# 64x64 array tiles for the chunk products of an RWKV-7 recurrence, and state products that alternate array halves

## The chip, the cores and the metric

The kernel runs on one core of a Trainium2 chip. The metric is the device time of one execution in microseconds. The core has TensorE (PE, matrix products; its weight loads are listed as PEld), VectorE (DVE), ScalarE (ACT), GpSimd (POOL) and SyncE (SP, which issues the DMAs). Products land in PSUM, a memory of 128 partitions in 8 banks of 512 fp32 words, and DVE or ACT bring them from there into the main on-chip memory.

## The reference

Two blocks stand in a row. The first is a recurrence over 768 tokens, for 4 batches of 8 heads with a state of 40 by 40 each; the second is a two-layer MLP with an exact gelu on its output, 3072 tokens of 320 values. All is float32.

```python
def _attn_ref(r, k, v, w, a, b):                      # (4, 8, 768, 40) each
    state = np.zeros((B, H, D, D), dtype=np.float32)
    for t in range(S):
        y[:, :, t] = np.einsum('bhd,bhde->bhe', rt, state)
        Sa = np.einsum('bhde,bhe->bhd', state, at)
        state_decay = state * wt[:, :, None, :] - np.einsum('bhd,bhe->bhde', Sa, bt)
        state = state_decay + np.einsum('bhd,bhe->bhde', vt, kt)
    return y

def _moe_ref(x, w_in, w_out):                         # (3072, 320), (320, 2048), (2048, 320)
    h = x @ w_in
    g = 0.5 * h * (1.0 + erf(h * inv_sqrt2))
    return g @ w_out
```

## The kernel before

The recurrence is cut into chunks of C = 64 tokens. A step handles one chunk of two batches: tokens of the first batch lie on partitions 0 to 63, those of the second on 64 to 127. There are 12 chunks and two pairs of batches, so 24 steps, which take turns between the pairs.

A step has two parts. `prep` (L256) needs no state: it scales a, k, b by the decays, turns five arrays so that heads and their columns lie on the partitions (`turn`, L236: four transposes into one PSUM bank and one copy), and multiplies them into token-by-token matrices (`products`, L247): P from bT and aT, A from kT and aT, RV from vT and rT. Then it inverts I + P by blocks, in six levels of z (L284), u (L293) and a transpose T (L301), with a DVE or ACT operation behind each. `chain` (L320) needs the state: X = A v plus a product with the state (`from_state`, L314), sa = the inverse times X, the new state out of Q (L348, ks with v and bs with sn), then M (`products` again, of snT and rT) and Y = RV ks + the state product + M bs.

Heads come in pairs: the first head of a pair lies on array rows 0 to 63, the second on rows 64 to 127, each with 40 values and 24 rows of zeros. `products` takes one half e of the rows after the other. For each it asks for a PSUM bank, multiplies the four pairs q on 64 rows with 128 weight columns and 128 streamed columns, and lets DVE copy the whole bank into place through a mask (L253). Weight columns and streamed columns are the 64 tokens of both batches, so half of each product pairs tokens of different batches; the mask leaves these out, and the tiles that they would go to hold zeros. Q is alike: its two halves e are the two batches, 64 rows each, and one half's eight products stand ahead of the other's. `from_state` uses all 128 rows and 64 weight columns, the two batches again one after the other.

PSUM is split into pools: `ps_prep` and `ps_chain` have three banks each, `ps_fc` two. A bank is free for its next user when the last reader of its contents is done.

The MLP of two chunks is written as a generator of parts (ph, L405, and po, L412), of which `parts` (L427) runs one behind each of the first eight yields of `prep`. Its passes are independent of the current step, and the framework orders each engine's instructions at build time by a model of their durations: it moves MLP passes into places where it expects TensorE to wait. On the chip, each engine's order is then fixed. For the first steps DVE also converts the MLP's weights from float64 words (L202 to L208).

Of the kernel before, what the change touches and what calls it, by code (L numbers as in the profile page):

```python
# [11 lines left out]
INT32 = mybir.dt.int32  # L12
# [5 lines left out]
#: As a float32, the high word of float64's 2 ** -126.  # L18
# [4 lines left out]
def kernel(  # L23
# [12 lines left out]
    """The recurrence in chunks of C = 64 tokens, all in float32.  # L36

    A step is one chunk of two batches, which lie on partitions 0-63 and 64-127; the
    two pairs of batches take turns. Within a chunk, with al[t] the sum of log w from
    the chunk's middle to (not including) t, per column e of the state,  # L40

        a'[t] = a[t] exp(al[t])    k'[s] = k[s] exp(-al[s + 1])    b'[s] = b[s] exp(-al[s + 1])

    and S the state at the chunk's start, decayed to its middle:

        sa[t] = S a'[t] + sum over s < t of v[s] (k'[s] a'[t]) - sa[s] (b'[s] a'[t])
        y[t] = exp(al[t]) (r[t] S + sum over s < t of (r[t] v[s]) k'[s] - (r[t] sa[s]) b'[s])

    The first is a unit triangular system (I + P) sa = X. Its inverse is built exactly,
    by blocks of 1, 2, 4 .. 32 that join in pairs. Arrays with heads on partitions hold  # L50
    two heads, each in 64 rows with zeros behind its D.

    al is at most 32 steps' log w, so the factors, and the products that the masks leave
    out, are finite for any decays above 0.26, and those of this kind are 0.85 to 0.95.
    """
# [22 lines left out]
    def bank(pool, name):  # L78
        return pool.tile([P, 512], FP32, tag=pool.name, name=name)
# [4 lines left out]
    def by_pair(t):  # L84
        return t.rearrange("p (q x) -> p q x", q=NP)
# [100 lines left out]
    def weights(dst, src):  # L186
        """The exponent loses its bias' difference, 7 * 128, in bits 7 to 9, and the 20 bits
        of mantissa in the high word move up; below float32's normal range it is zero. The
        low word, times the power of two that it counts in, is added: one rounding."""
# [57 lines left out]
    def products(pool, dst, lT, rT, mask):  # L247
        for e in range(2):
            rows = slice(e * HP, (e + 1) * HP)
            pt = by_pair(bank(pool, "prod_ps"))  # L250
            for q in range(NP):
                nc.tensor.matmul(pt[:, q], lT[rows, q], rT[rows, q], start=True, stop=True)  # L252
            nc.vector.copy_predicated(  # L253
                dst[:, e], mask.bitcast(INT32).unsqueeze(1).to_broadcast([P, NP, P]), pt)

    def prep(i):  # L256
# [17 lines left out]
        # Tt is the transpose of (I + P)^-1 within blocks of m tokens, and T that of Tt.  # L274
# [39 lines left out]
    def from_state(o, xT, st):  # L314
        for e in range(2):
            rows = slice(e * C, (e + 1) * C)
            for q in range(NP):
                mm(o[rows, 2 * q:2 * q + 2], xT[:, q, rows], st(e, q), False)

    def chain(i):  # L320
# [18 lines left out]
        if c < NCH - 1:  # L339
            f = f_ring(i)  # L340
            for e in range(2):
                rows = slice(e * HP, (e + 1) * HP)
                nc.gpsimd.tensor_tensor(f[rows, :, :, e], half_w[rows, :, 1],
                                        decays[i + NG][2][rows, :, 0], ALU.mult)
            new = st_ring(i)
            for e in range(2):
                rows = slice(e * C, (e + 1) * C)
                Q = bank(ps_chain, "Q")[:, :NP * 2 * D].rearrange("p (q x d) -> p q x d", q=NP, x=2)  # L348
                for q in range(NP):
                    hs = slice(2 * q, 2 * q + 2)  # L350
                    for n, (l_, r_) in enumerate(((ks, v_), (bs, sn))):
                        mm(Q[:, q], l_[rows, hs].rearrange("p h d -> p (h d)"), r_[rows, hs, :D],
                           q == 0 and n == 0)
                ns = new[:, e, :, :, :D]
                fb = f[:, :, e].unsqueeze(3).to_broadcast([P, NP, 2, D])
                if state is None:
                    nc.vector.tensor_tensor(ns, Q, fb, ALU.mult)
                else:
                    nc.vector.tensor_tensor(ns, Q, st[:, e, :, :, :D], ALU.add)
                    nc.vector.tensor_tensor(ns, ns, fb, ALU.mult)  # L360
# [62 lines left out]
    # Parts of the MLP stand between the levels of the inverse, as the tensor engine would  # L423
    # wait there for others.
# [62 lines left out]
```

## Time and profile before

| | |
|---|---|
| time, median of 2 runs | 1968.95 us (1968.61 to 1969.3) |
| span of the profiled execution, first to last instruction | 1934.2 us |
| TensorE busy, matmuls | 1882.7 us |
| VectorE busy | 547.5 us |
| ScalarE busy | 385.4 us |
| GpSimd busy | 127.6 us |

The profiled execution has no time of its own beside its span; the runs' median is 34.8 us above that span. On the page, line numbers such as L252 are those of the kernel above. A line can be that of a helper: L88 is the helper `mm`, which issues the products of X, sa, Q and Y, and they are told apart by the tile that they write. The shape of a product is written as rows * weight columns, then rows x streamed columns; "x16" is a count. The granted clock is the share of TensorE's full clock that the chip let through. The chain is followed back from the last instruction to what released each one.

### The profile page before, as it was taken

What the parts mean: (1) busy time and instruction counts of PE and PEld (TensorE: products, weight loads), DVE (VectorE), ACT (ScalarE), POOL (GpSimd) and SP (SyncE); (2) the same over time, 40 slices, a digit from 0 to 9 for tenths busy, and PEclk for the clock granted to TensorE, in tenths of its full rate; (3) what the DMA queues carried; (4) which work ended last, traced back from release to release, by engine and by line L of the source; (5) the groups of instructions that cost most, each with busy time, mean ns of one, the idle gap of its engine ahead of it and who ended that gap; (6) DMA issues with size and microseconds to landing.
All of it is one profiled execution on the core that took longest, in us unless ns stands there. A gap on an engine that the chain in (4) does not pass through costs nothing.

```text
span 1934.2 us, 28576 instructions
## 1 busy us (share of the span) xinstructions
PE 1882.7 (97%) x12648; PEld 1611.3 (83%) x12648; DVE 547.5 (28%) x1002; ACT 385.4 (20%) x652; POOL 127.6 (7%) x214
## 2 busy tenths in 40 slices
PE   6888899999999999999999999999999999999999
PEld 6888887888888888788788888888888888888785
DVE  2464732322222222133132232222222222232210
ACT  3111112221212212222122122221221221221200
POOL 4121210000000000000000000000000000000000
PEclk9555759987998996998998899899999999999999
DMA  5241310100001001011010010010100100000000
GB/s 87 50 92 49 79 21 8 22 18 11 15 15 21 11 18 21 1 25 24 1 25 14 11 21 17 13 22 7 18 15 11 17 5 11 4 1 7 1 4 11
DMA packets 160905, 39.84 MB, mean 21 GB/s; under 512 B 153424, under 2 KB 156816, under 8 KB 160784
## 3 DMA queue, kind: packets, MB, share of 16 engines
q1 hardware_dynamic: 160784, 38.03, 10.0%
q8 instruction: 99, 1.62, 0.3%
q14 instruction: 22, 0.18, 0.0%
HBM read 34.08 MB, written 3.93 MB: 20 GB/s over the span
## 4 chain that ended last, share of the span: by engine, by line
PE 96%; DVE 2%; POOL 1%; issue 0%; ACT 0%; POOLq 0%
PE ph L405 16%; PE z_ps L284 14%; PE u_ps L293 13%; PE po L412 11%; PE prod_ps L252 9%; PE Y L88 8%; PE T_ps L301 6%; PE Q L88 5%; PE X L88 3%; PE sa L88 2%; PE turned_ps L375 1%; PE sums L226 1%; PE snT_ps L239 1%; PE aT_ps L239 1%; PE kT_ps L239 1%; PE cum L218 1%
## 5 line engine op out<-in xcount | busy, mean ns | idle before, releaser
L405 PE MATMUL ph<-xT,w_in_sb 128*128 128x256 f32 (+1 forms) x1152 | 333.2, 412 | 0.0
L293 PEld LDWEIGHTS u_ps<-zs,T 128*128 128x128 f32 x1920 | 245.1, 206 | 42.4 <-issue 40.3
L293 PE MATMUL u_ps<-zs,T 128*128 128x64 f32 x1920 | 254.7, 290 | 17.5 <-DVE zs L287 17.5
L405 PEld LDWEIGHTS ph<-xT,w_in_sb 128*128 128x128 f32 (+1 forms) x1152 | 188.4, 190 | 99.2 <-issue 86.7
L284 PEld LDWEIGHTS z_ps<-Tt,P 128*128 128x128 f32 x1920 | 244.4, 205 | 19.3 <-issue 14.6
L287 DVE TENSOR_TENSOR zs<-z_ps,level_m 128x512 f32<-128x512 f32 x144 | 99.5, 691 | 553.0 <-PE z_ps L284 553.0
L302 ACT COPY T<-T_ps 128x512 f32<-128x512 f32 x240 | 130.0, 588 | 608.7 <-PE T_ps L301 606.9
L284 PE MATMUL z_ps<-Tt,P 128*128 128x64 f32 x1920 | 249.9, 287 | 0.0
L412 PE MATMUL po<-w_out_sb,gt 128*128 128x320 f32 x768 | 238.9, 443 | 0.0
L412 PEld LDWEIGHTS po<-w_out_sb,gt 128*128 128x128 f32 x768 | 135.2, 192 | 38.5 <-issue 0.3
L296 DVE TENSOR_TENSOR Tt<-u_ps,Tt 128x512 f32<-128x512 f32 x120 | 83.0, 692 | 287.9 <-PE u_ps L293 287.9
L301 PEld LDWEIGHTS T_ps<-ident,Tt 128*128 128x128 f32 x960 | 114.6, 148 | 42.3 <-issue 19.9
L301 PE MATMUL T_ps<-ident,Tt 128*128 128x128 f32 x960 | 137.6, 290 | 12.4 <-DVE Tt L296 12.1
L407 ACT ACTIVATE gt<-ph 128x512 f32<-128x512 f32 x96 | 57.3, 597 | 392.8 <-PE ph L405 392.8
L88 PE MATMUL Q<-sn,bs 64*128 64x80 f32 x352 | 73.2, 328 | 0.0
L277 POOL COPY Tt<-ident 128x1024 f32<-128x1024 f32 x24 | 24.9, 1038 | 684.2 <-PE sa L88 664.8
L88 PE MATMUL Q<-v,ks 64*128 64x80 f32 x352 | 69.8, 320 | 0.0
L88 PEld LDWEIGHTS Q<-sn,bs 64*128 64x128 f32 x352 | 61.8, 231 | 4.7 <-issue 4.3
L376 ACT COPY turned<-turned_ps 128x512 f32<-128x512 f32 x44 | 24.5, 588 | 197.2 <-PE turned_ps L375 197.2
L88 PE MATMUL Y<-bs,M 128*128 128x40 f32 x384 | 62.5, 333 | 0.0
L88 PEld LDWEIGHTS Y<-bs,M 128*128 128x128 f32 x384 | 59.7, 244 | 2.6 <-issue 1.2
L88 PE MATMUL Y<-ks,RV 128*128 128x40 f32 x384 | 59.0, 322 | 0.0
(113 smaller groups left out, 1917.4 us busy)
## 6 DMA issues: line engine op xcount, KB each, us to landing
gt<-in_moe_w_out_dram SPq DMA_DIRECT2D x16, 320.0 KB, 2.9
w_raw<-in_w_dram SPq DMA_DIRECT2D x48, 80.0 KB, 2.8
k_raw<-in_k_dram SPq DMA_DIRECT2D x48, 80.0 KB, 2.8
a_raw<-in_a_dram SPq DMA_DIRECT2D x48, 80.0 KB, 2.8
b_raw<-in_b_dram SPq DMA_DIRECT2D x48, 80.0 KB, 2.8
v<-in_v_dram SPq DMA_DIRECT2D x48, 80.0 KB, 2.6
r<-in_r_dram SPq DMA_DIRECT2D x48, 80.0 KB, 2.8
gt<-in_moe_w_in_dram SPq DMA_DIRECT2D x12, 320.0 KB, 3.1
```

The source lines that it names most:

```text
L88: nc.tensor.matmul(o, lhsT, rhs, start=first, stop=True, skip_group_check=True)
L239: nc.tensor.transpose(by_pair(pt)[:, q], src(q), ident)
L252: nc.tensor.matmul(pt[:, q], lT[rows, q], rT[rows, q], start=True, stop=True)
L284: nc.tensor.matmul(cols(z[:, h]), Pm[:, e, q], right(ident if n == 0 else Tt[:, h]), start=True, stop=True)
L287: nc.vector.tensor_tensor(zs, z, level_m[:, n].unsqueeze(1).to_broadcast([P, H, C]), ALU.mult)
L293: nc.tensor.matmul(u[:, h], T[:, h], zs[:, h], start=True, stop=True)
L296: nc.vector.tensor_tensor(Tr, cols(u.rearrange("p h c -> p (h c)")), Tr, ALU.add)
L301: nc.tensor.transpose(pt[:, q], Tt[:, e * NP + q], ident)
L302: nc.scalar.copy(T[:, e * NP:(e + 1) * NP], pt)
L405: nc.tensor.matmul(ph[:, x], w_in_sb[:rows, kt, (f + x) * P:(f + x + 1) * P], xt[:rows, kt], start=kt == 0, stop=kt == NK - 1)
L407: nc.scalar.activation(gt[:, f:f + 2], ph, ACT.Gelu)
L412: nc.tensor.matmul(po, gt[:, f, j * P:(j + 1) * P], w_out_sb[:, f], start=f == 0, stop=f == NF - 1)
```

## The change

In `products`, both banks are asked for at the start. Each product of 64 rows by 128 weight columns by 128 streamed columns becomes two of 64 by 64 by 64, one for each batch g, and the blocks that pair different batches are not computed any more. Rows e and weight columns g choose one of four 64x64 tiles of the array, and the four take turns within a pair q. The two masked copies of 128 partitions by 512 become four of 64 partitions by 256, behind all matmuls.

In `from_state` the loops change places, so that the two batches alternate. In `chain`, both banks of Q are asked for at the start, the loop over e goes innermost, and the operations on the new state stand behind all of Q's products. All other lines of the difference remove comments.

```diff
     def products(pool, dst, lT, rT, mask):
+        pts = [by_pair(bank(pool, "prod_ps")) for _ in range(2)]
+        for q in range(NP):
+            for g in range(2):
+                own = slice(g * C, (g + 1) * C)
+                for e in range(2):
+                    rows = slice(e * HP, (e + 1) * HP)
+                    nc.tensor.matmul(pts[e][own, q, own], lT[rows, q, own], rT[rows, q, own],
+                                     start=True, stop=True, skip_group_check=True)
         for e in range(2):
-            rows = slice(e * HP, (e + 1) * HP)
-            pt = by_pair(bank(pool, "prod_ps"))
-            for q in range(NP):
-                nc.tensor.matmul(pt[:, q], lT[rows, q], rT[rows, q], start=True, stop=True)
-            nc.vector.copy_predicated(
-                dst[:, e], mask.bitcast(INT32).unsqueeze(1).to_broadcast([P, NP, P]), pt)
+            for g in range(2):
+                own = slice(g * C, (g + 1) * C)
+                nc.vector.copy_predicated(
+                    dst[own, e, :, own],
+                    mask[own, own].bitcast(INT32).unsqueeze(1).to_broadcast([C, NP, C]), pts[e][own, :, own])
...
     def from_state(o, xT, st):
-        for e in range(2):
-            rows = slice(e * C, (e + 1) * C)
-            for q in range(NP):
+        for q in range(NP):
+            for e in range(2):
+                rows = slice(e * C, (e + 1) * C)
                 mm(o[rows, 2 * q:2 * q + 2], xT[:, q, rows], st(e, q), False)
...
             new = st_ring(i)
-            for e in range(2):
-                rows = slice(e * C, (e + 1) * C)
-                Q = bank(ps_chain, "Q")[:, :NP * 2 * D].rearrange("p (q x d) -> p q x d", q=NP, x=2)
-                for q in range(NP):
-                    hs = slice(2 * q, 2 * q + 2)
-                    for n, (l_, r_) in enumerate(((ks, v_), (bs, sn))):
-                        mm(Q[:, q], l_[rows, hs].rearrange("p h d -> p (h d)"), r_[rows, hs, :D],
+            Qs = [bank(ps_chain, "Q")[:, :NP * 2 * D].rearrange("p (q x d) -> p q x d", q=NP, x=2)
+                  for _ in range(2)]
+            for q in range(NP):
+                hs = slice(2 * q, 2 * q + 2)
+                for n, (l_, r_) in enumerate(((ks, v_), (bs, sn))):
+                    for e in range(2):
+                        rows = slice(e * C, (e + 1) * C)
+                        mm(Qs[e][:, q], l_[rows, hs].rearrange("p h d -> p (h d)"), r_[rows, hs, :D],
                            q == 0 and n == 0)
+            for e in range(2):
+                Q = Qs[e]
                 ns = new[:, e, :, :, :D]
...
```

More of the change, by code (lines that the diff above doesn't have):

```diff
@@ L345, in chain @@
             new = st_ring(i)
-            for e in range(2):
-                rows = slice(e * C, (e + 1) * C)
-                Q = bank(ps_chain, "Q")[:, :NP * 2 * D].rearrange("p (q x d) -> p q x d", q=NP, x=2)
-                for q in range(NP):
-                    hs = slice(2 * q, 2 * q + 2)
-                    for n, (l_, r_) in enumerate(((ks, v_), (bs, sn))):
-                        mm(Q[:, q], l_[rows, hs].rearrange("p h d -> p (h d)"), r_[rows, hs, :D],
-                           q == 0 and n == 0)
+            Qs = [bank(ps_chain, "Q")[:, :NP * 2 * D].rearrange("p (q x d) -> p q x d", q=NP, x=2)
[6 more added lines that the diff above has]
+                        mm(Qs[e][:, q], l_[rows, hs].rearrange("p h d -> p (h d)"), r_[rows, hs, :D],
+                           q == 0 and n == 0)
+            for e in range(2):
+                Q = Qs[e]
                 ns = new[:, e, :, :, :D]
```

## The prediction

> **What bounds the kernel now.** I read the page first, for the engine that carries the time, its clock and the chain that ended last.
>
> ```profile
> span 1934.2 us, 28576 instructions
> PE 1882.7 (97%) x12648; PEld 1611.3 (83%) x12648; DVE 547.5 (28%) x1002; ACT 385.4 (20%) x652; POOL 127.6 (7%) x214
> ...
> PEclk9555759987998996998998899899999999999999
> ...
> PE 96%; DVE 2%; POOL 1%; issue 0%; ACT 0%; POOLq 0%
> PE ph L405 16%; PE z_ps L284 14%; PE u_ps L293 13%; PE po L412 11%; PE prod_ps L252 9%; PE Y L88 8%; PE T_ps L301 6%; PE Q L88 5%; PE X L88 3%; PE sa L88 2%; PE turned_ps L375 1%; PE sums L226 1%; PE snT_ps L239 1%; PE aT_ps L239 1%; PE kT_ps L239 1%; PE cum L218 1%
> ```
>
> TensorE is the bound: 96% of the chain, with DVE at 28%. The products (L252) are 9% of it, Q 5%, and X and Y, of which the state products are a third, 11%. The row of the clock says that TensorE often ran slowed. Two stretches of the table by windows (time, then busy us of PE, PEld, DVE, ACT, POOL, then the granted clock) show where:
>
> ```profile
> 0.00:300.00 300.00, 259.82 (x1402) 243.51 (x1403) 141.39 (x325) 54.67 (x90) 64.21 (x119) 0.64 0.28 62
> 300.00:1934.00 1634.00, 1622.85 (x11248) 1367.78 (x11246) 406.10 (x678) 330.69 (x562) 63.41 (x95) 0.95 0.07 13
> ```
>
> The clock takes two values here, 1.0 and 0.5, so 0.64 and 0.95 mean some 216 and 163 us at half clock, 380 in all. Behind the start TensorE is busy 99%.
>
> Then the chain of waits in order of time (start, us, work), for one step at full clock, one at half clock and the levels of the inverse:
>
> ```profile
> 1578.75 2.90 PE Q L88 x28
> ...
> 1583.22 1.64 PE prod_ps L252 x16
> 1584.86 4.85 PE Y L88 x48
> ...
> 1590.93 1.64 PE prod_ps L252 x16
> 1592.57 0.59 PE kT_ps L239 x4
> 1593.16 0.44 PE vT_ps L239 x4
> 1593.60 0.51 PE rT_ps L239 x4
> 1594.11 3.06 PE prod_ps L252 x31
> 1597.16 1.93 PE z_ps L284 x16
> ```
>
> ```profile
> 1047.29 5.42 PE Q L88 x28
> ...
> 1056.70 3.02 PE prod_ps L252 x16
> ```
>
> ```profile
> 1625.87 2.16 PE po L412 x8
> 1628.03 1.73 PE z_ps L284 x16
> ...
> 1633.88 0.71 PE X L88 x12
> ```
>
> Each fp32 product stands as two passes (a weight load and a matmul): 8 products of a call are 16 rows. Prices of a pass: po streams 320 columns in 2.16 / 8 = 0.270 us, 0.84 ns a column. z streams 64 but loads 128 columns of weights, and takes 1.73 / 16 = 0.108 us, again 0.84 ns a column, of the load. So a pass costs the longer of its load and its stream. Behind products z costs 1.93: a change of tile shape is 0.2 us. At half clock the products' 1.64 becomes 3.02.
>
> Whether two halves of the array work at once is seen in the timeline of Q, whose two halves meet only in the middle:
>
> ```profile
> 1579.86 0.27 PE L88 MATMUL Q<-v,ks 64*128 64x80 f32 x1
> 1579.87 0.33 PE L88 MATMUL Q<-sn,bs 64*128 64x80 f32 x1
> 1579.97 0.27 PE L88 MATMUL Q<-v,ks 64*128 64x80 f32 x1
> ```
>
> They do: a pass of the other half starts 0.01 us behind the first, and the first half goes on 0.11 later. The overlap is short today because one half's passes all stand ahead of the other's.
>
> **The change, part by part** (times at full clock, per step; 24 steps, of which 22 have a state).
>
> Products: 16 passes of 128 columns become 32 of 64 by 64, on four tiles. A pass is then 64 x 0.84 = 0.054 us, a tile has 8, so four tiles side by side need 0.43. With the change of shape (0.2) and the first load (0.1) a call is 0.73 at best. No row shows four tiles at once. From above, the densest row is X with 12 passes in 0.71, 0.059 a pass, so 32 would be 1.9. I take 0.9: two passes 0.01 us apart in Q put it near the lower end. P and M thus save 1.64 - 0.9 = 0.74 each. A and RV, back to back, go from 3.06 to about 1.7 and save 1.36. Together 2.84 x 24 = 68 us.
>
> Q: in pairs, the 28 passes are 14 x 0.108 + 0.3 = 1.8 instead of 2.90: 1.1 x 22 = 24 us. The load of 128 columns decides, not the 80 streamed. If nothing overlapped beyond today the saving would be 0.
>
> State products: of Y's 48 passes 32 cost 32 x 0.108 = 3.46 and two changes of shape 0.4, which leaves 1.0 for 16 passes of 80 columns. In pairs they take 8 x 0.067 + 0.1 = 0.64 there, saving about 0.25 beside the rest, and X about 0.2 of its 0.71 and the four passes ahead of it. 0.45 x 22 = 10 us; bounds 0 and 0.55 a step.
>
> Sum at full clock 102 us. At half clock each saving doubles; 380 us of 1934 are at half clock, so +20%: 122.
>
> What comes back is the mask. Rows of DVE by shape (busy us, mean ns):
>
> ```profile
> L253 DVE COPY_PREDICATED P<-lower,prod_ps 128x512 f32<-128x512 int32 x48 | 33.0, 727 | 22.4 <-PE prod_ps L252 22.3
> L241 DVE COPY snT<-snT_ps 128x512 f32<-128x512 f32 x24 | 16.6, 692 | 9.0 <-PE snT_ps L239 7.6
> L389 DVE COPY xT<-x_ps 128x256 f32<-128x256 f32 x24 | 10.2, 424 | 24.3 <-PE x_ps L387 24.2
> ```
>
> ```profile
> 1592.06 1.34 DVE L253 COPY_PREDICATED P<-lower,prod_ps 128x512 f32<-128x512 int32 x2 [0.47 <-PE prod_ps L252]
> 1595.23 1.33 DVE L253 COPY_PREDICATED A<-upper,prod_ps 128x512 f32<-128x512 int32 x2 [1.83 <-PE prod_ps L252]
> ```
>
> 256 elements fewer save 692 - 424 = 268 ns, so a copy of half the size is some 460 ns, and 4 of them, overlapped as the pair is (1.34 for two), about 1.5 us. As DVE work that is 96 x 0.2 = 19 us more on an engine at 28%: nothing. But today the first copy starts while TensorE still fills the second bank (1592.06, 0.5 us before the products end at 1592.57). Afterwards both banks are filled to the last pass, so all four copies follow the products. `ps_prep` has three banks: vT needs one that the copies of P free (0.9 us behind P's end, kT covers 0.45), rT the second (1.6 behind), and the second bank of RV is one of A's (0.9 behind A's end). TensorE runs in order, so what stands behind them waits: about 0.8 us a step at P and 0.9 at RV. In the chain, both halves of Q now end together, and four operations on st (L359, L360) can stand ahead of the snT copy that M waits for: up to 1 us. M itself is covered by Y's first 32 passes. Uncovered, 2.7 x 24 = 65 us. The cover is the MLP: pieces of po and ph are already placed into each wait of the levels, 8 po passes (2.16) where the copies of T need about 1.2, so it has some room, yet it is used up every four steps. I take half as uncovered: 33.
>
> 122 - 33 = 89 us off the span, 1845; the medians are 35 us above it (1968.95 against 1934.2), so **1880 us**.
>
> Moved matmuls touch no DMA queue, and SP and POOL issue the same as before.
>
> **What the clock does** is the least certain term. Neighbouring windows of 3.41 us, and what a window that lost the clock and one that kept it held:
>
> ```profile
> 1206.81:1210.22 3.41, 2.85 (x28) 2.68 (x27) 2.29 (x4) 0.58 (x1) 0.00 (x0) 1.00 0.44 72
> 1210.22:1213.63 3.41, 3.41 (x25) 3.16 (x25) 0.00 (x0) 0.00 (x0) 0.86 (x1) 0.50 0.02 5
> 1585.70:1589.10 3.40, 3.40 (x39) 3.26 (x38) 0.00 (x0) 0.00 (x0) 0.86 (x1) 1.00 0.02 5
> ```
>
> ```profile
> L252 PE MATMUL prod_ps<-rT,snT 64*128 64x128 f32 x16 | 1.7, 285 | 0.6 <-DVE snT L241 0.6
> L88 PE MATMUL Y<-ks,RV 128*128 128x40 f32 x11 | 1.5, 296 | 0.0
> L239 PE MATMUL bT_ps<-ident,bs 128*128 128x128 f32 x1 | 0.3, 273 | 0.0
> ```
>
> ```profile
> L88 PE MATMUL Y<-bs,M 128*128 128x40 f32 x13 | 1.6, 284 | 0.0
> L88 PE MATMUL Y<-ks,RV 128*128 128x40 f32 x10 | 1.3, 283 | 0.0
> L88 PE MATMUL Y<-turned,rT 128*64 128x80 f32 x16 | 1.1, 239 | 0.0
> ```
>
> Count streamed columns, a pass on 64 rows as half: the first has 16 x 128 / 2 + 11 x 40 + 128 = 1592, at 0.84 ns 39% of the window, and the next ran at half. The second has 23 x 40 + 16 x 80 = 2200, 54%, and kept the clock. With a pass of 64 weight columns as half too it would have 1560, fewer than the first, and yet it stayed: rows count, weight columns don't. [...]
>
> After the change the first window's products end 0.74 sooner and seven more Y passes (280 columns) move in. If each tile counts by its rows, it holds 1872, 46%, and the clock stays. If two tiles beside each other on the same rows count once, it holds 512 + 440 + 128 + 280 = 1360, 33%, and it falls. No row tells which. I take the half clock's share as unchanged.
>
> **Rivals.**
> The clock eats it (same or slower): tiles on the same rows count once, and more windows fall. Each us at half clock costs half a us of full-clock work, so 89 us are gone with 178 us more of it, 380 growing to 558; from 256 more the kernel is slower by 2%. With 300 more, 15 in each step behind the start, it is 1880 + 150 = 2030. For it: the count above, and windows at 39% lie just on the edge. Against: products and Q become denser.
>
> Passes come no faster than the densest row, 0.059 us: a product call is 1.9, P and M lose 0.25 each and A with RV 64 x 0.059 - 3.06 = 0.72. That is 29 us lost against 34 x 1.2 = 41 won, 1957. For it: no row is denser over a whole call; against it the 0.01 us in Q. [...]
>
> The tiles don't run beside each other: 32 x 0.054 + 0.3 = 2.0 a call, within 0.1 of the rival just told, and it is counted with it.
>
> **How the numbers follow.** Forecast 0.57 (1840 with all waits covered, 1915 with none and a little more half clock). Clock 0.28, of which 0.17 lie between 1930 and 2009 and 0.11 beyond. Passes too slow 0.15, some of it just below 1930. A difference under 2% (39 us) is about what can't be told from no change. Faster 0.60, same 0.29, slower 0.11. The range is 1840 to 1975: it takes in the second rival and most of the first's middle.
>
> **What would show it.** Products at 0.9 a call in the chain of waits; 2.0 is the second rival. Q x28 at 1.8. Waits of PE for DVE at vT, rT, RV and snT, or po and ph there instead. The mean clock (0.90 now, from the two windows at the top): about 0.90 confirms, 0.86 or less (558 us at half clock of some 1930) means that the first rival took it, and then the prediction is wrong though each part may have become shorter.

## The result, and the profile after

| | before | after |
|---|---|---|
| time, median | 1968.95 us (2 runs) | 1821.45 us (1816.02 to 1826.89, 2 runs) |
| ratio, 95% interval | | 0.9245 [0.9175, 0.9315] |

The changed kernel is faster by 7.5%, and 19 us below the lower end of the predicted range. The lines of its page that answer to those shown of before: span, TensorE, granted clock in 40 slices, and the chain that ended last.

```profile
span 1824.9 us, 31928 instructions
PE 1763.7 (97%) x14184; PEld 1486.6 (81%) x14184; DVE 577.6 (32%) x1194; ACT 389.5 (21%) x652; POOL 128.5 (7%) x214
...
PEclk8555557999997999997999997998899999998999
...
PE 95%; DVE 2%; POOL 1%; issue 1%; ACT 0%; DVEq 0%; POOLq 0%
```

TensorE is still the bound, with 1536 more passes and 119 us less busy time. A step at full clock, from the chain of waits of the changed kernel (start, us, work):

```profile
1486.94 1.72 PE Q L88 x28
...
1490.77 0.96 PE prod_ps L254 x42
1491.73 2.96 PE Y L88 x34
...
1495.15 1.49 PE Y L88 x14
...
1498.83 1.08 PE po L422 x4
...
1500.78 1.41 PE prod_ps L254 x47
1502.19 0.74 PE po L422 x2
1502.92 0.61 PE prod_ps L254 x16
1503.54 0.74 PE po L422 x2
1504.27 1.73 PE z_ps L291 x16
```

Q's 28 passes take 1.72 (2.90 before), Y's 48 take 4.45 (4.85). 42 product passes, the 32 of M and 10 of P, stand in 0.96. A and RV take 1.41 + 0.61 = 2.02 (3.06), and po passes, MLP work, stand where RV has to wait for a bank. The waits for masks have hardly any idle time left in them. These are TensorE's waits for DVE ahead of products, by releaser (us in all, times, longest):

```profile
PE prod_ps L254 <- DVE A L259: 5.3, 3, 4.0
...
PE prod_ps L254 <- DVE P L259: 2.1, 2, 1.4
...
PE prod_ps L254 <- DVE snT L241: 0.2, 1, 0.2
```

That is 7.6 us in the whole execution. One of the four groups of mask copies shows the price of a copy, 440 ns where some 460 were forecast:

```profile
L259 DVE COPY_PREDICATED A<-upper,prod_ps 64x256 f32<-64x256 int32 x96 | 42.2, 440 | 35.2 <-PE prod_ps L254 33.7
```

**Two accounts.** Span times granted clock is the work at full clock (with TensorE's idle time in it); 2 x (1 - clock) x span is the time spent at half clock, and half of that is lost. The records of the clock in the traces of the two kernels hold two values alone, 1.0 and 0.5. By these definitions the two always add up to the span. The page of before was an execution with an unusually high clock (1934.2 us), and a second profile of the same kernel, taken for the experiments, is the better partner. The cores view of that one, then of the changed kernel:

```profile
core 0: 1966.5 us, clock 0.887
```

```profile
core 0: 1824.9 us, clock 0.904
```

Before: 1744 us of work and 444 at half clock. After: 1650 and 350. So of the 141.6 us between the two spans 94 are work, and 47 are the worth of 94 us less at half clock. Windows of the same two executions show where the clock came back:

```profile
0.00:300.00 300.00, 259.41 (x1314) 243.97 (x1315) 136.15 (x316) 52.28 (x85) 63.47 (x119) 0.60 0.28 61
300.00:1966.00 1666.00, 1655.19 (x11336) 1395.88 (x11334) 411.43 (x687) 333.74 (x567) 64.16 (x96) 0.94 0.07 13
```

```profile
0.00:300.00 300.00, 251.80 (x1561) 234.84 (x1561) 143.73 (x346) 54.76 (x89) 65.06 (x119) 0.58 0.28 61
300.00:1825.00 1525.00, 1511.91 (x12625) 1251.74 (x12623) 433.90 (x848) 334.69 (x563) 63.40 (x95) 0.97 0.08 14
```

The first 300 us stay as slow as they were (0.60 and 0.58). Behind them the half-clock time falls from 2 x 0.06 x 1666 = 200 us to 92. In the middle of the execution three falls of the clock in every four steps (436.1, 528.3 and 603.4 us before) have become one (558.7 after).

Ratios are formed from undisturbed runs alone; the kernel before ran at 1936 to 1982 us in nearly all of its others, so where experiments with different neighbours are set side by side below, it is by span and clock.

### The profile page after: what moved, and what is told of

Read it like the earlier page. It is cut to its first block, busy times and chain, and to the rows that moved or that the text cites. A ratio compares the mean times of both kernels' runs of the same rounds, so it can differ in the third digit from the quotient of the medians.

```text
span 1824.9 us, 31928 instructions
## 1 busy us (share of the span) xinstructions
PE 1763.7 (97%) x14184; PEld 1486.6 (81%) x14184; DVE 577.6 (32%) x1194; ACT 389.5 (21%) x652; POOL 128.5 (7%) x214
## 4 chain that ended last, share of the span: by engine, by line
PE 95%; DVE 2%; POOL 1%; issue 1%; ACT 0%; DVEq 0%; POOLq 0%
PE ph L415 17%; PE z_ps L291 16%; PE u_ps L300 13%; PE po L422 12%; PE Y L88 7%; PE T_ps L308 7%; PE prod_ps L254 5%; PE X L88 4%; PE Q L88 3%; PE sa L88 3%; PE turned_ps L385 1%; PE sums L226 1%; PE kT_ps L239 1%; PE snT_ps L239 1%; PE aT_ps L239 1%; PE cum L218 1%
## 5 line engine op out<-in xcount | busy, mean ns | idle before, releaser
L415 PE MATMUL ph<-xT,w_in_sb 128*128 128x256 f32 (+1 forms) x1152 | 337.2, 412 | 0.0
L291 PEld LDWEIGHTS z_ps<-Tt,P 128*128 128x128 f32 x1920 | 248.9, 209 | 16.1 <-issue 12.9
L291 PE MATMUL z_ps<-Tt,P 128*128 128x64 f32 x1920 | 254.3, 290 | 0.0
L422 PE MATMUL po<-w_out_sb,gt 128*128 128x320 f32 x768 | 243.4, 444 | 0.0
L88 PEld LDWEIGHTS Y<-ks,RV 128*128 128x128 f32 x384 | 54.6, 227 | 1.9
L88 PEld LDWEIGHTS sa<-xs,Tt 128*128 128x128 f32 x384 | 52.7, 216 | 2.0 <-DVE Tt L303 0.2
L259 DVE COPY_PREDICATED A<-upper,prod_ps 64x256 f32<-64x256 int32 x96 | 42.2, 440 | 35.2 <-PE prod_ps L254 33.7
```

The source lines that it names most:

```text
L88: nc.tensor.matmul(o, lhsT, rhs, start=first, stop=True, skip_group_check=True)
L291: nc.tensor.matmul(cols(z[:, h]), Pm[:, e, q], right(ident if n == 0 else Tt[:, h]), start=True, stop=True)
L415: nc.tensor.matmul(ph[:, x], w_in_sb[:rows, kt, (f + x) * P:(f + x + 1) * P], xt[:rows, kt], start=kt == 0, stop=kt == NK - 1)
L422: nc.tensor.matmul(po, gt[:, f, j * P:(j + 1) * P], w_out_sb[:, f], start=f == 0, stop=f == NF - 1)
```

## The experiments

Theory: two separate gains, fewer and shorter passes (work), and less time at half clock, because denser windows of 3.41 us keep the clock (before, one with columns streaming for 39% of it was followed by half clock, one with 54% was not). The rivals are named at each. Work and half clock are us, from the profile's span and clock.

| kernel | median, us | span, clock of its profile | work | at half clock |
|---|---|---|---|---|
| before (second profile) | 1968.45 | 1966.5, 0.887 | 1744 | 444 |
| changed | 1821.45 | 1824.9, 0.904 | 1650 | 350 |
| products only | 1882.18 | 1883.2, 0.893 | 1682 | 403 |
| Q and state products only | 1915.98 | 1911.5, 0.895 | 1711 | 401 |
| masks copied twice | 1854.61 | 1851.6, 0.902 | 1670 | 363 |
| tile after tile | 1879.85 | 1875.1, 0.905 | 1697 | 356 |
| one row half first | 1812.52 | 1808.8, 0.920 | 1664 | 289 |
| before, wider streams | 1887.00 | 1881.6, 0.926 | 1742 | 278 |
| changed, wider streams | 1816.51 | 1817.9, 0.899 | 1634 | 367 |
| changed, dense work in the first two preparations | 1759.32 | 1797.1, 0.931 | 1673 | 248 |
| changed, dense work at Q and Y every four steps | 1800.41 | 1791.2, 0.925 | 1657 | 269 |
| both of these, three preparations | 1755.59 | 1750.0, 0.980 | 1715 | 70 |

The recorded clock does not fit the span in every execution: a second one with masks copied twice has 1853.6 us at 0.973, where the table's has 1851.6 at 0.902, and one execution each of products only, tile after tile and one row half first also stands 16 to 98 us of work above the others of its kernel. Why this is so is open; none of them is in the table.

**Do the times stand above the spans by a fixed amount?** The changed kernel again, unaltered, and later the kernel before, for its profile.

> The changed kernel once more, beside five rounds of the kernel before. Theory 1: the 35 us between the median of before and its profiled span are no fixed cost; every run lies about 2 us above its own span, and the runs of before at 1969 have a lower mean clock than the 0.904 of the profiled one. Then before gives 1936 to 1970 with clocks of 0.88 to 0.91, after 1815 to 1830, and the difference of the spans at equal clock is about 109 us. Theory 2: the 35 us belong to the kernel before as a fixed cost that the change removed. Then before's spans are 1934 at 0.904 in every run while its times are 1969.

> The kernel before once more, with its trace. Theory 1 (its profile on the page was of an execution with an unusually high clock): span 1966 to 1980 at a mean clock of 0.88 to 0.887, about 450 us at half clock, of which some 200 lie behind the first 300 us where the page's execution had 163. Theory 2 (a fixed cost): 1934 at 0.904.

Six runs of the changed kernel gave a median of 1815.28 us (1813.44 to 1832.77), ratio 0.9216 [0.9184, 0.9249]; the second profile of before ran in 1968.45 us with a span of 1966.5. Every run lies some 2 us above its own span. The 35 us between the first page and the median were clock (0.904 there, 0.880 to 0.887 in the eleven runs of the kernel before that ran beside the first of these), not a fixed cost. The same eleven runs spent 444 to 475 us at half clock, the six of the changed kernel 322 to 370, at 1742 to 1744 and 1646 to 1651 us of work: the fall of the half-clock time does not hang on the two profiles chosen above.

**One half of the change alone.** First `products` as in the change with Q and `from_state` as before, then the reverse.

```diff
     def products(pool, dst, lT, rT, mask):
...
-                nc.tensor.matmul(pt[:, q], lT[rows, q], rT[rows, q], start=True, stop=True)
+                    nc.tensor.matmul(pts[e][own, q, own], lT[rows, q, own], rT[rows, q, own],
+                                     start=True, stop=True, skip_group_check=True)
...
```

```diff
     def from_state(o, xT, st):
-        for e in range(2):
-            rows = slice(e * C, (e + 1) * C)
-            for q in range(NP):
+        for q in range(NP):
+            for e in range(2):
+                rows = slice(e * C, (e + 1) * C)
...
```

> Only the products stand as 64x64 tiles; Q and the state products are as before. Theory 1 (the parts add up by their TensorE time: products 75 us, Q 33, state products 13 of 121): about 1969 - 0.62 x 147 = 1878, range 1865 to 1900, mean clock 0.90. Theory 2 (a good part of the gain is the clock's, which the thin Q keeps low): the parts do not add up, time above 1905 with a mean clock of 0.89 or less.

> Only Q and the state products alternate; the products are as before. Theory 1: 0.38 of the gain, about 1969 - 56 = 1913, range 1900 to 1930, Q x28 at 1.7 us. Theory 2 (the denser Q lifts the clock): below 1900 with a mean clock above 0.92.

Products only: ratio 0.9542 [0.9509, 0.9574]; Q and state only: 0.9705 [0.9672, 0.9738]. By the table they take out 62 and 33 us of work, 95 together against 94, and 41 and 43 us of half clock, 84 against 94. The parts add up in work, and in half clock within its spread from run to run. A call of products alone in the chain of waits, from the kernel with products only:

```profile
1608.58 0.62 PE prod_ps L254 x32
```

32 passes in 0.62 us, 19 ns a pass. The 0.73 that the prediction gave as the best had 0.2 us for the change of tile shape in it, which the chain books with the rows beside the products (the four ph passes ahead take 1.25 here and 1.06 further on), so by these rows a call with it is about 0.8.

**Does it need the turns between the tiles?** All four products of one tile, then the next.

```diff
-        for q in range(NP):
+        for e in range(2):
+            rows = slice(e * HP, (e + 1) * HP)
             for g in range(2):
                 own = slice(g * C, (g + 1) * C)
-                for e in range(2):
-                    rows = slice(e * HP, (e + 1) * HP)
+                for q in range(NP):
...
```

> The changed kernel with the products' loops in the order tile, then pair: all four products of a tile stand behind one another, the tiles don't take turns. Theory 1 (a tile holds some four passes ahead, what is behind them waits): a call grows from about 0.7 to about 1.2 us, 96 calls give 40 us, time 1840 to 1870. Theory 2 (the order is free, since TensorE looks far enough ahead): within 10 us of the changed kernel.

Time 1879.85 us, ratio 0.9662 [0.9575, 0.9749]: more was lost than either number allowed for. The same two places in its chain of waits:

```profile
1601.38 2.06 PE prod_ps L254 x51
...
1611.73 2.90 PE prod_ps L254 x64
```

40 and 45 ns a pass, where the changed kernel has 23 (0.96 for 42) and 30 (1.41 for 47) in the same places: passes on one tile in a row overlapped less than passes on different tiles in turn. That a tile holds some four passes ahead was the author's assumption; no run shows a number. The half-clock time is as in the changed kernel (356 and 350); the loss is work.

**The mask copies.** Each of the four copies is issued twice, and in another kernel the halves of the rows follow each other, so that the first two copies start while TensorE fills the second bank.

```diff
+                for _ in range(2):
                     nc.vector.copy_predicated(
                         dst[own, e, :, own],
...
```

```diff
-        pts = [by_pair(bank(pool, "prod_ps")) for _ in range(2)]
-        for q in range(NP):
-            for g in range(2):
-                own = slice(g * C, (g + 1) * C)
-                for e in range(2):
-                    rows = slice(e * HP, (e + 1) * HP)
-                    nc.tensor.matmul(pts[e][own, q, own], lT[rows, q, own], rT[rows, q, own],
-                                     start=True, stop=True, skip_group_check=True)
         for e in range(2):
+            rows = slice(e * HP, (e + 1) * HP)
+            pt = by_pair(bank(pool, "prod_ps"))
+            for q in range(NP):
+                for g in range(2):
+                    own = slice(g * C, (g + 1) * C)
+                    nc.tensor.matmul(pt[own, q, own], lT[rows, q, own], rT[rows, q, own],
+                                     start=True, stop=True, skip_group_check=True)
             for g in range(2):
...
```

> The changed kernel with each masked copy made twice, so that the masks of a call take about 3.3 us instead of 1.8. Theory 1 (MLP passes cover the waits for the masks, with room left): less than 25 us above the changed kernel, PE idle time before products and transposes below 15 us in all, and more po and ph passes between P, A and RV. Rival (the cover is used up, as the prediction took for half of it): three waits of 1.4 us in each of 24 steps open up, 100 us, or half of that, 50, above the changed kernel.

> The changed kernel with the products of one row half, two column tiles in turn, and their two masked copies ahead of the other half's, one bank after the other. Theory 1 (the waits for masks are covered, so an earlier first mask wins nothing, and two tiles in place of four cost some 0.3 us a call): 1815 to 1850, not below the changed kernel. Rival (the waits for masks still cost): 10 to 30 us below it, at 1785 to 1805.

Doubling adds 4 x 96 x 0.44 = 169 us to DVE and 39 us to the time (1854.61 against 1815.28, run together), between what the two theories gave. 20 of them are work; half clock is 363 us against 322 to 350 in most runs of the changed kernel. The MLP's passes cover most of a wait, but not one twice as long. With one row half ahead of the other the time is 1812.52 us (1810.83 to 1812.98), ratio 0.9308 [0.9249, 0.9367], not to be told apart from the changed kernel. It has 14 us more work and 33 to 61 us less half clock than the changed kernel in most of its runs. The earlier copies win no idle time; TensorE now waits for A's masks once in each of the 24 steps, 9.9 us in all where the changed kernel has 5.3 in three waits:

```profile
PE prod_ps L254 <- DVE A L258: 9.9, 24, 1.8
```

**Which count of columns fits the clock?** A kernel by itself, which leaves the whole computation out: four series of short bursts, each burst between two DVE copies that TensorE waits for, with dense work ahead of each series. The bursts are, in this order, 8 passes on each of two 64-column tiles in turn (all 128 rows), 8 passes on one such tile, 16 passes on one tile, and 8 passes on each of four 64x64 tiles.

```diff
+    def pair_burst():
+        for q in range(4):
+            for e in range(2):
+                rows = slice(64 * e, 64 * e + 64)
+                mm(banks[0][rows, 80 * q:80 * q + 80], wts[:, rows], src[:, 80 * q:80 * q + 80])
...
```

> None of the reference is computed, the output is zeros. Four series of 24 bursts on TensorE, a DVE copy between bursts, each series behind 50 full products of 512 columns that bring the clock up. Bursts: pairs of 64-column tiles side by side (8 passes of 80 columns on each), one 64-column tile (8 passes), one 64-column tile (16 passes), four 64x64 tiles (8 passes of 64 columns on each). With a burst about every 1.7 us, the streamed time, summed over tiles by their rows, is 62%, 32%, about 47% and about 55% of the time; with tiles on the same rows counted once it is 31%, 32%, 47% and 28%. If tiles on the same rows count once, the clock falls to half in series 1, 2 and 4 and stays up in series 3. If each tile counts, it falls in series 2 alone.

One burst of each series at full clock from its chain of waits, with the DVE copies between the bursts left out (the chain follows half of the last series' passes), and then the series by windows with the granted clock in the third column from the right:

```profile
50.09 0.80 PE bank L33 x16
```

```profile
141.04 0.78 PE bank L33 x8
```

```profile
236.60 1.33 PE bank L33 x16
```

```profile
328.46 0.71 PE bank L33 x16
```

```profile
55.00:93.00 38.00, 23.80 (x288) 19.46 (x286) 17.44 (x36) 0.00 (x0) 0.50 0.00 1
...
145.00:186.00 41.00, 26.07 (x159) 21.25 (x157) 18.68 (x39) 0.00 (x0) 0.50 0.00 0
...
236.00:278.00 42.00, 26.42 (x320) 23.19 (x320) 19.58 (x41) 0.00 (x0) 1.00 0.00 1
...
333.00:366.00 33.00, 27.60 (x548) 24.38 (x548) 17.10 (x36) 0.00 (x0) 0.50 0.01 2
```

With the gap a burst of pairs returns every 1.57 us, one of 8 single passes every 1.55, 16 single passes every 2.10, four tiles every 1.48. At 0.84 ns a column the streams are, by tiles added up (four tiles at half, for their rows): 16 x 80 x 0.84 / 1570 = 68%, 35%, 51% and 58% of the time. Only the 51% kept the clock, and 68% and 58% lost it. Counting tiles on the same rows once makes it 34%, 35%, 51% and 29%, which is in order: 35% and less lost the clock, 51% kept it. So in these four series the count that fits leaves weight columns out, and a second tile beside the first on the same rows adds nothing to it. The share of time in which a burst lasts at all (51%, 50%, 63% and 48%) would sort these four as well, but not the kernel's windows: there the clock fell with TensorE busy for 3.41 of 3.41 us. In the first series the gaps were 0.8 us and the clock fell within the first bursts (one takes 0.80 us at 53.23 and 1.36 at 56.92), so no longer idle stretch stood ahead of the fall.

**Is that what moves the clock in the kernel?** X, sa and Y's products with A, the inverse, RV and M stream 64 columns a head, 24 of them zeros that lie in the rings anyway (for xs, the input of sa, a ring is added). Their passes, with 40 streamed columns, take as long as those of z with 64 (14 of Y 1.49 us and 16 of z 1.73, 0.106 and 0.108 a pass); both load 128 weight columns, and the load bounds them. Once in the changed kernel, once in the kernel before.

```diff
...
-            mm(o[:, h], m_of(h), rhs[:, h, :D], first and h == 0)
+            mm(o[:, h], m_of(h), rhs[:, h], first and h == 0)
...
```

> The changed kernel, with X, sa and Y's products by A, RV, M and the inverse streaming 64 columns a head (24 of them zeros that the rings hold already) in place of 40. The passes there are bound by the load of their 128 weight columns, so the work takes as long; only the density of what streams rises. Theory (the clock goes by streamed columns in a window): half-clock time falls from 320 to 350 us to 250 to 300, time 1780 to 1805 us. Rival (the clock goes by something else, or these streams aren't what lets it fall): within 10 us of the changed kernel's 1815, or above by what wider streams cost (16 x 5 passes of 20 ns a step, 20 us).

> The kernel before, with the same wider streams in X, sa and Y, and nothing of the change. Theory (the clock goes by streamed columns in a window): half-clock time falls from 450 us by 40 to 100 us, time 1915 to 1950 us with no work taken out. Rival: within 10 us of the kernel before in the same call, or above by up to 20 us.

The kernel before goes to 1887.00 us (its own runs beside it had a median of 1972.88), ratio 0.9721 [0.9662, 0.978], by nothing but zeros in its streams: its work stays (1742 us) and its half clock drops from 444 (384 to 471 in the runs beside it) to 278. That is more than theory gave. The changed kernel gains nothing (1816.51, against 1815.28 and 1821.45 above), where 10 to 35 us were expected. Its work is some 14 us lower, which no run explains, and its half clock is 348 to 367 us, so it is not less: the falls have moved. In the changed kernel those at 558.7, 838.6 and 1118.5 us stand behind sa and the start of Q. The window before the first of them, and that before the fall of the wider kernel at 554.5:

```profile
L88 PE MATMUL sa<-xs,Tt 128*128 128x40 f32 x16 | 2.0, 283 | 0.0
L226 PE MATMUL sums<-halves,logw 128*128 128x4 f32 x7 | 0.9, 253 | 0.0
L239 PE MATMUL aT_ps<-ident,as 128*128 128x128 f32 x4 | 0.7, 286 | 0.0
L88 PE MATMUL Q<-v,ks 64*128 64x80 f32 x4 | 0.5, 303 | 0.0
L239 PE MATMUL bT_ps<-ident,bs 128*128 128x128 f32 x1 | 0.3, 306 | 0.0
```

```profile
L292 PE MATMUL z_ps<-Tt,P 128*128 128x64 f32 x15 | 1.8, 275 | 0.0
L301 PE MATMUL u_ps<-zs,T 128*128 128x64 f32 x8 | 1.1, 284 | 0.9 <-DVE zs L295 0.9
```

Both hold 36% of their time in streamed columns (1468 and 1472). With wider streams the clock no longer falls behind sa. It falls in the inverse instead, where z and u have no MLP passes between them; the falls at 837.8, 1117.7 and 1401.0 us stand in such places too.

The next kernels add two or three dense matmuls (identity by 384 constant columns, read by nobody) where the changed kernel's trace has them: in the first preparations, which run beside no MLP part, and in the step of every four whose Q stands without MLP passes.

```diff
+    def warm(n):
+        t = bank(ps_fc, "warm")
+        for _ in range(n):
+            nc.tensor.matmul(t[:, :len(LEVELS) * C], ident, level_m.rearrange("p n c -> p (n c)"),
+                             start=True, stop=True)
...
             for n, _ in enumerate(prep(i + 1)):
+                if i < NG:
+                    warm(3)
                 parts(n < 8)
...
```

> The changed kernel, with three added matmuls (the identity against 384 constant columns, into a bank that nobody reads) after each of the twelve parts of the inverse in the first three steps, where no MLP part fills: 108 added matmuls that take no part in the result. Theory: the first 300 us of the changed kernel run at half clock (0.58 granted) because what streams there is too sparse, and not because the chip is busy or warm; with dense work between, the clock stays up there (granted 0.85 or more in that stretch), and the 125 us that half the clock costs come back but for the added work: some 1720 to 1780 us. Rival: the half clock there has another cause (the start, the transfers), or DVE and ACT set the pace of the inverse anyway: the granted clock stays under 0.7 and the added 108 passes of 0.6 to 1.2 us cost 60 to 120 us: 1870 us or more.

Median 1759.32 us, ratio 0.9043 [0.9002, 0.9084]; the profile is of the longest of its five runs, and the median one had a span of 1757.3 at 0.957, so 1682 us of work and 151 at half clock. NG is 2, so it was two preparations and 72 matmuls, not three and 108. Windows of it, while the additions last and behind them:

```profile
50.00:100.00 50.00, 48.21 (x433) 38.56 (x433) 44.50 (x104) 10.74 (x18) 14.55 (x17) 1.00 0.51 113
...
150.00:200.00 50.00, 44.67 (x303) 39.96 (x302) 30.65 (x75) 6.83 (x12) 9.02 (x9) 0.64 0.22 59
```

The additions last to 161 us. The clock is 1.00 in the first 100 us and 0.97 in the next 50; from 50 to 100 us 433 passes run, where the changed kernel has 251 and a clock of 0.52. A first attempt on the later falls, beside these additions:

```diff
+            if not fill:
+                warm(2)
             new = st_ring(i)
...
```

> The kernel with the added matmuls in the first three steps, and two more of them ahead of Q and two ahead of Y in each step that finds no MLP part waiting (they take no part in the result). Theory: after the first 300 us the changed kernel's clock falls once in about 280 us, in the step without MLP parts, at Q or just behind it, and stays at half for 20 us; with 1.2 us of dense work ahead of Q and of Y it does not fall there. Some 10 us of half clock a fall come back, for 2.5 us of added work: 1730 to 1755 us, granted clock 0.96 or more. Rival: the falls stay or move behind Y, and the added work costs 15 to 20 us: 1765 to 1785 us.

It gave 1767.44 us (1749.28 to 1784.54), ratio 0.9142 [0.8996, 0.9288], no gain. Its trace shows why it decides nothing: all 168 added passes start before 191 us, so the later falls got none. The next two kernels place them by the step's number, ahead of Q and of Y; the first has no other additions, the second has them in three preparations as well.

```diff
+            if i % 4 == 2:
+                warm(2)
             new = st_ring(i)
...
```

> The changed kernel with two added matmuls (identity by 384 constant columns, no part in the result) ahead of Q and two ahead of Y in every fourth step, the third of each four, where its trace shows the clock falling at sa and Q (558.7, 838.6, 1118.5 us), and nothing added at the start: 22 matmuls, 27 passes' worth of 14 us at full clock. Theory (a 3.4 us stretch with too few streamed columns lets the clock fall, and only the step without MLP work beside Q has one left): these falls go, the granted clock behind 300 us rises from 0.97 to 0.99 or more, 60 to 90 us less half clock there, so 15 to 30 us less time for the clock and 14 more for the work: 1795 to 1815. Rival (the falls belong to the step or to the place of the windows, not to what streams): they stay, granted clock 0.97, 1825 to 1835.

> The same additions at Q and Y in every fourth step, and three added matmuls after each of the twelve parts of the inverse in the first three preparations that run beside no MLP part (the run before with such an addition had them in two). Theory: the half clock from 150 to 250 us of that run (granted 0.57 to 0.64) goes too, 35 to 40 us of half clock, 18 us of time for some 10 to 20 of added work that partly stands in waits, and the falls at Q go: 1725 to 1755. Rival: no better than that run's 1759, as the added work costs what the clock gives.

At Q and Y only: 1800.41 us (1791.56 to 1809.31), ratio 0.9135 [0.9082, 0.9188], and behind the start:

```profile
300.00:1791.00 1491.00, 1483.49 (x12615) 1223.50 (x12611) 433.19 (x847) 333.73 (x562) 63.37 (x95) 1.00 0.08 14
```

A clock of 1.00 instead of 0.97: with dense work in them, these stretches kept the clock, except for some 10 us (of the 269 us at half clock 258 lie in the first 300, at 0.57). Both together gave 1755.59 us (1751.96 to 1764.68), ratio 0.8923 [0.888, 0.8966]. That is the fastest version, though not to be told apart from the 1759.32 of two preparations: half clock is down to 70 us, and 65 us of added work stand against it.

## Why the prediction was wrong

**The sizes at full clock were right in sum.** It was 102 us: products 68, Q 24, state products 10. Products alone took out 62 of work, with the mask waits already in it, Q and state products 33 where 34 were forecast. Q came as put, 1.72 for 1.8, and so did a call of products, 0.62 and the change of shape for 0.9. A and RV took 2.02 for 1.7, with MLP passes between, some 8 us in 24 steps.

**The rivals on passes fell.** Passes do run faster than 0.059 us and the tiles do run beside each other (19 ns a pass) when they take turns; tile after tile, at 40 to 45 ns, goes about half of the way back to these rivals.

**The waits for masks were mis-sized.** "I take half as uncovered: 33" measured 7.6 us of idle time: MLP passes stand in the waits. The waits were put at the right banks; the cover was better than half. That is some 25 us.

**The step that failed is "I take the half clock's share as unchanged".** In the two profiles with a typical clock, half clock went from 444 to 350 us, worth 47 us, where the +20% gave 20. With the masks' 25 these 27 are the 52 us by which the gain of 89 missed the 141 between the spans. The predicted and the measured median are 59 us apart (1880 and 1821); most of the remaining 6 is that the profiled run of the changed kernel lay 5 us above its median. Both errors went the same way, so they added up.

**Why the clock rose although a second tile added nothing to the count.** The rival's count was right in the experiment: pairs of tiles on the same rows lost the clock (34% counted once, 68% added up), where one tile at 51% kept it. It went wrong in what it let into the window. It filled the room in the changed window with Y passes alone (33%, and a fall). In the trace, shorter parts let denser neighbours in. Two windows of the kernel before, the first of which held sa, Q and aT:

```profile
524.90:528.32 3.42, 3.42 (x31) 3.12 (x31) 1.42 (x3) 1.04 (x3) 1.66 (x3) 1.00 0.00 0
528.32:531.73 3.41, 3.41 (x21) 3.27 (x21) 1.03 (x3) 1.67 (x2) 0.00 (x0) 0.50 0.29 48
```

```profile
L88 PE MATMUL sa<-xs,Tt 128*128 128x40 f32 x13 | 1.6, 283 | 0.0
L88 PE MATMUL Q<-sn,bs 64*128 64x80 f32 x6 | 1.3, 294 | 0.0
L88 PE MATMUL Q<-v,ks 64*128 64x80 f32 x8 | 1.2, 287 | 0.0
L239 PE MATMUL aT_ps<-ident,as 128*128 128x128 f32 x4 | 0.7, 287 | 0.0
```

13 x 40 + 14 x 80 / 2 + 4 x 128 = 1592 columns, 39% of the window, and the next ran at half. Now a window of the changed kernel with M's and P's products and the start of Y, grouped the same way. This is the place of the prediction's window at 1206.81 us (M and the start of Y, 39%), behind which before had a fall:

```profile
L88 PE MATMUL Y<-ks,RV 128*128 128x40 f32 x16 | 2.0, 284 | 0.0
L254 PE MATMUL prod_ps<-rT,snT 64*64 64x64 f32 x32 | 0.7, 221 | 0.0
L415 PE MATMUL ph<-xT,w_in_sb 128*128 128x256 f32 x2 | 0.7, 432 | 0.0
L254 PE MATMUL prod_ps<-bT,aT 64*64 64x64 f32 x20 | 0.6, 228 | 0.0
L88 PE MATMUL Y<-turned,rT 128*64 128x80 f32 x4 | 0.4, 258 | 0.0
```

It has room for M, part of P and two ph passes beside Y. Counted once, the products are 52 x 64 / 4 = 832 columns and the state products 160; with 640 of Y and 512 of ph that is 2144, 53% of 3.41 us, and the clock stayed.

These are single windows, and the lists take in passes that lie across an edge. The same count over every window at full clock, a pass going to the window in which it starts, gives for the second profile of before: 16 falls behind windows of 31.5 to 36.6%, and 420 windows of 37.0% and more without a fall. For the page's execution of before it gives 13 falls behind 33.1 to 39.0% and 436 windows without one, of 37.0% and more (8 of them below the 39.0); one more fall, at the end of TensorE's work, stands behind a window in which nothing streams. For the changed kernel it gives 11 falls behind 19 to 39% and 411 windows without one, of 36% and more. With the second tile counted too, falls in the changed kernel would stand behind windows of up to 52%, with 73 windows below that which kept the clock (15 below the 39% when tiles on the same rows count once).

**The 35 us** between median and span was a difference of clock between executions. As it was added back to the same median it did no harm to the sum; but taking the half clock from that one page (380 us) where 444 to 475 is typical left the clock's share too small, by some 3 us.

**What stays open**: why executions of one kernel differ in their half-clock time (329 to 475 us in nearly all runs of before). That the place of the windows against the program matters is likely from what stands at the end, but no run tried it.

## What to carry to other kernels

Keep two accounts for TensorE, work at full clock and time at half clock, and take them from several executions; a change can move both. Let small products on separate tiles of the array take turns: here a pass took 19 ns with neighbours in the order on different tiles, and 40 to 45 tile after tile. Look for sparse stretches: in the three executions counted, every fall stood behind a window of 3.41 us in which columns streamed for at most 39% of the time. Shorten such a stretch, stream more columns where the weight load is the limit (0.106 us a pass with 40 columns, 0.108 with 64), or put dense work into it: zeros in the streams made the kernel before 2.8% faster (ratio 0.9721 [0.9662, 0.978]), and dense filler the changed one by some 57 us (1816.51 to 1759.32, run together, the first with wider streams).

## What the runs showed of the hardware

- Four 64x64 tiles in turn take 32 fp32 passes in 0.62 us, 19 ns a pass, where one tile after the other takes 40 to 45 (51 passes in 2.06 us, 64 in 2.90).
- The clock fell in the first series of bursts with TensorE never idle for more than 0.8 us, and in the kernel before behind windows with no idle time at all (busy 3.42 of 3.42 us). Windows of 3.41 us lost it in which columns stream for at most 36.6% (before, second profile), 39.0% (before, the page's execution) or 39% (changed) of the time, and no window above that did in the same execution, at 0.84 ns a column, with rows as weight, weight columns ignored and tiles on the same rows counted once.
- All changes of the clock in the page's execution of before, and all in that of the changed kernel, lie on a grid of 3.413 us (to 5 ns). In that of before a fall returns at 425.2, 735.8 and 1046.4 us, 310.61 us apart, which is 91.0 windows; four steps take 90.98 to 90.99 windows there, so program and grid keep in step. In the changed kernel a fall stands at 558.7, 838.6 and 1118.5, 82.0 windows apart, while four steps take 82.05 to 82.10, and the next one stands elsewhere (1265.3).
